# Output products of a small expert block two F tiles behind their relus, and its gathers issued from a later step

## The chip, the cores and the metric

The kernel runs on one core of a Trainium2 chip. The metric is the device time of one execution in microseconds (us). The kernel before was run three times: 393.76, 395.10 and 396.24 us, median 395.1 us. One further execution was profiled. The core has five engines, each with its own queue of instructions in program order: PE (TensorE, matrix products, its weight loads listed as PEld), DVE (VectorE), ACT (ScalarE), POOL (GpSimd) and SP (SyncE, which only issues DMAs here). They synchronise through semaphores.

## The reference

An RWKV-5 attention is followed by a mixture of experts with one expert per token.

```python
# attention: B, H, S, D = 4, 8, 768, 48; state starts at 0
for t in range(S):
    cur = einsum('bhd,bhe->bhde', u * k[t], v[t])
    y[t] = einsum('bhd,bhde->bhe', r[t], state + cur)
    state = w * state + einsum('bhd,bhe->bhde', k[t], v[t])
x = y as (B, S, H * D)                          # 3072 tokens of 384 values
# experts: E, F = 8, 1024
logits = x @ w_gate                             # (B, S, 8)
local = sigmoid(x @ w_local)
for b, s in order:
    e = argmax(logits[b, s]) if s == 0 or local[b, s] < 0.5 else previous e
    p = softmax(logits[b, s])
    out[b, s] = p[e] * (relu(x[b, s] @ w1[e]) @ w2[e])
```

Which expert a token goes to depends on the tokens before it in its batch, so the assignment is computed on the chip, and the tokens are then gathered by expert. Everything is in float32.

## The kernel before, in words

**Attention.** 16 items (4 batches by 4 pairs of heads) pass through a software pipeline (`Attention.run`), whose loop counter n goes from 0 to 16. When all heads of a batch are done, ACT issues a DMA that stores the batch's rows of x into a DRAM tile, `x_d`. Batches 0 and 1 (group 0) are complete at n = 8. In the steps that follow, the router works out the expert and the slot of each token of group 0 beside the attention of batches 2 and 3. At n = 15, `router.head` writes `gid0`, the row numbers of the first tokens of experts 0 and 1, and the callback `heads()` issues gathers for them.

**Gathers.** `Experts.gather(i)` issues one indirect DMA on POOL's queue for each 128 slots of block i: from `x_d`, by the row numbers in `gid`, into a tile `xg` (L1032). There are six `xg` tiles in turn, and a seventh gather has to wait until the tile it overwrites has been read by PE.

**Expert blocks.** `Experts.run` goes through ten blocks ("units"). Blocks 0 and 1 are small: 192 slots each for experts 0 and 1, filled from group 0 alone (`EARLY = 2`, `HEAD = 192`), so they can be computed while the router treats group 1. Blocks 2 to 9 take the eight experts by size, with 448, 424, 392, 376, 352, 336, 232 and 192 slots. Those with at least 336 slots use a scheme with fewer products (`eleven` and `seven`) and are called large here.

For a small block the loop goes over the eight F tiles m of 128 hidden features. `hidden(i, m)` computes three products into one of two PSUM buffers `h` (L1059), and ACT applies the relu into `hT` (L1062). `output(i, m)` multiplies `hT` by the second weights, three products that accumulate over m in PSUM tiles y0 to y2 (L1143). Four `hT` tiles are live at a time. `lag` says how many F tiles the output products stand behind the hidden products; it is 1 for blocks 0 and 1. Each step also runs a piece of the router for group 1 (`routing(s)`, with s = 8 i + m), and in the last steps `turn` transposes gathered tokens of the next block on PE (L1045) with a copy by DVE (L1046). The routing steps that matter here: s = 1 turns the keys of group 1 (`r.keys`), s = 8 computes row numbers of all tokens and gathers the first large block, s = 10 and s = 12 sum gates on PE (`summed`, L788), s = 14 makes one tiny product for a flag.

**Block 1** is followed by a large block (`following` is true for it alone). Its last two output products are not issued in its own loop: they are put in a list, `todo`, from which the large block takes them to fill PE. Output product 5 is issued after the loop, and output products 0 to 4 in the loop, each directly after the hidden product of the next tile. The gather of block 3 also follows the loop.

**Order.** The schedule is manual: every engine executes its instructions in the order in which the Python code emits them, and waits are derived from the tiles, buffers and DRAM regions that an instruction shares with earlier ones. Weights of block i are fetched into one of two buffers, blocks 0 and 2 onwards by SP, block 1 by ACT (`self.fetch(1, self.nc.scalar)` in block 0, step 1).

Of the kernel before, what the change touches and what calls it, by code (L numbers as in the profile page):

```python
# [26 lines left out]
DK, FK = D // P, F // P  # L27
# [9 lines left out]
EARLY = 2  # L37
# [925 lines left out]
class Experts:  # L963
# [43 lines left out]
    def bank(self, name):  # L1007
        if self.both:
            self.tp.reverse()
        return self.tp[0]  # L1010
# [291 lines left out]
    def routing(self, s):  # L1302

        r, bank = self.router, self.bank
        if s == 0:
            r.experts_of(1)
            r.shares(1)
            r.gates(0)
        if s == 1:
            r.keys(1, bank("kp1"))  # L1310
            r.runs(1)
            r.powers(1)
        if s == 2:
            r.turn_runs(1, bank("rp1"))
        if s == 3:
            r.last(1, bank("bc1"))
            r.one_hot(1)
        if s == 4:
            r.counts(1, [bank("rk1"), bank("tt1")])
            r.ranks(1)  # L1320
            r.blocks()
            r.slots(1)
            r.columns(1)
            r.numbers(1)
            r.places(1, 0)
            r.places(1, 1)
        if s == 5:
            self.fetch(EARLY, self.nc.sync)
        if s == 7:
            r.summed(1, 0)  # L1330
            r.copied(0)
        if s == 8:
            r.tokens(bank("tb1"))
            self.gather(EARLY)
            r.gates(1)
            r.weights(0)
            r.weights(1)
        if s == 10:
            r.summed(0, 1)
        if s == 12:  # L1340
            r.summed(1, 1)
            r.copied(1)
        if s == 13:
            self.flag(0)
        if s == 14:
            self.flag(1, bank("fp"))
        if s == 2 * FK:
            r.ends(bank("tb2"))

    def run(self, att, flag, ready):  # L1350
        self.flag, self.spare, self.hs = flag, att.late, None
        n = len(self.units)
        sends = []
        yb = [self.yps.tile([P, 512], F32, name=f"y{d}") for d in range(DK)]
        att.logits(B - 1, yb[0])
        for j in range(len(self.units[0]["rows"])):
            self.turn(0, j)
        att.token_logits(B - 1, yb[2])
        self.warm(2)
        self.router.powers(0)  # L1360
        later, todo, behind = [], [], None

        def fill(k=None):
            while todo and k != 0:
                todo.pop(0)()
                k = k and k - 1

        def take():
            nonlocal behind
            if behind:  # L1370
                (k, j), behind = behind, None
                todo.extend(self.seven(k, j))
                if j == FK // 2 - 1:
                    todo.append(lambda: joined(k))

        def joined(k):
            later.extend(self.join(k))
            if "yT" in self.units[k]:
                sends.extend((k, r) for r in range(2, len(self.units[k]["rows"])))
            if k + 2 < n:  # L1380
                self.fetch(k + 2, self.nc.sync)

        def drained(i):
            self.drain(i)
            sends.extend((i, j) for j in range(len(self.units[i]["rows"])))

        def then(k):
            for _ in range(min(k, len(later))):
                later.pop(0)()

        for i in range(n):
            u = self.units[i]
            after = len(self.units[i + 1]["rows"]) if i + 1 < n else 0
            following = i + 1 < n and self.units[i + 1]["seven"]
            if i == EARLY:
                self.fetch(i + 1, self.nc.sync)
                self.hs = self.spare.tile([P, 2, 3, BLOCKS[0] // 2], F32, name="hs", tag="xT")
            if u["seven"]:

                at = ["m0", "m1" if i == EARLY else "a1", "a2" if i == EARLY else "m1", "m2" if i == EARLY else "a2"][4 - after:]  # L1400

                def slot(name):
                    if (i, name) == (EARLY, "a1"):
                        self.routing(2 * FK)
                    elif name in at:
                        self.turn(i + 1, at.index(name))
                    elif sends and (i, name) > (EARLY, "b"):
                        self.send(*sends.pop(0))

                for j in range(FK // 2):  # L1410
                    if behind:
                        self.factors(*behind)
                        self.sums(*behind)
                        take()
                    then(4)
                    if j == 3 and following:
                        later.extend(self.token_sums(i + 1))
                    self.eleven(i, j, fill, lambda: slot(f"a{j}"), then)
                    behind = i, j
                    if j == 1:  # L1420
                        self.weight_sums(i, 1)
                        if i == EARLY:
                            later.extend((self.router.exceeded, lambda: self.router.halves(0), lambda: self.flag(2)))
                    if i == EARLY + 1 and j == 1:
                        later.append(lambda: self.router.halves(E - 1))
                    if j == 2 and following:
                        self.weight_sums(i + 1, 0)
                    if j == 3 and i + 2 < n:
                        self.gather(i + 2)
                    fill(max(len(todo) - 3, 0))  # L1430
                    slot(f"m{j}")
                    fill()
                continue

            lag = 3 if i and self.units[i - 1]["seven"] else 1
            for m in range(FK):
                if following and m == FK - 1:
                    self.turn(i + 1, after - 1)
                if m == 0 and behind:
                    self.factors(*behind)  # L1440
                    self.sums(*behind)
                self.hidden(i, m)
                if m == 0:
                    take()
                    fill()
                while later and m == 1:
                    later.pop(0)()
                if i == 0 and m == 0:
                    att.turn(B * HP - 1, [self.bank("tp") for _ in range(2)])
                if sends and m >= 1 and i > EARLY:  # L1450
                    self.send(*sends.pop(0))
                if m and i == n - 1:
                    self.rows(m - 1)
                elif m >= lag and not (following and m > FK - 3):
                    self.output(i, m - lag)
                if i <= EARLY:
                    self.routing(i * FK + m)
                if i == 0 and m == 1:
                    self.fetch(1, self.nc.scalar)
                if following and m == FK - 3:  # L1460
                    self.weight_sums(i + 1, 0)
                if m >= FK - after and not (following and m == FK - 1):
                    self.turn(i + 1, m - (FK - after))
            if EARLY <= i + 1 and i + 2 < n:
                self.gather(i + 2)

            if following:
                self.output(i, FK - 3)
                for step in self.token_sums(i + 1):
                    step()  # L1470
                self.both = False
                todo.extend(lambda i=i, m=m, d=d: self.output(i, m, (d,)) for m in range(FK - 2, FK) for d in range(DK))
                todo.append(lambda i=i: drained(i))
            elif i < n - 1:
                for m in range(FK - lag, FK):
                    self.output(i, m)
                drained(i)
        self.rows(FK - 1)
        self.send_rows(0)
        self.half_rows()  # L1480
        ready()
        self.send_rows(1)
# [44 lines left out]
def kernel(  # L1527
# [12 lines left out]
    nc = tc.nc  # L1540
# [28 lines left out]
    with ExitStack() as st, tc.manual_schedule():  # L1569
        ro = st.enter_context(tc.tile_pool(name="ro", bufs=1))  # L1570
        mpp = st.enter_context(tc.tile_pool(name="mpp", bufs=1, space=PSUM))
        router = Router(tc, ro, mpp, lt, mask, ident, gid, sid, gate, over[:, 0:1])
        ex = Experts(tc, st, x_d, w1, w2, out, ident, router)
        att = Attention(tc, st, rk_d, kv_d, vT_d, x_d, w_t, wp_d, kept, ident, lt, router.mp)
        att.run(router, lambda: ex.fetch(0, nc.sync), lambda: [ex.gather(i) for i in range(EARLY)])
        ex.open(st)
        router.open(1, st.enter_context(tc.tile_pool(name="ro1", bufs=1)))

# [91 lines left out]
```

## Time and profile before

| | |
|---|---|
| Median of three runs | 395.1 us (393.76 to 396.24) |
| Profiled execution | 395.21 us, of which span 393.5 us |
| Mean granted PE clock | 0.993 |
| PE busy | 375.9 us, 96% of the span |
| PEld busy | 332.1 us, 84% |
| DVE busy | 242.2 us, 62% |
| POOL busy | 143.9 us, 37% |
| ACT busy | 106.8 us, 27% |
| Hidden products of small and last blocks (L1059) | 192 records, 37.9 us |
| Output products (L1143) | 144 records, 29.2 us |
| Gathers (L1032) | 29, 30.4 us |

The span runs from the first to the last instruction of the program; the execution's own time has 1.7 us more around it. Block 0 runs from about 122 to 141 us of the span, block 1 from 141 to 161 us. A line of a timeline reads: start, duration, engine, source line, operation, output and inputs with shapes, how many were merged; in square brackets the idle time of the engine before it and what ended that. One float32 matmul of the program appears as two records, so that the three products of an F tile are six records. "Remote" as a releaser means that the profile could not tell which instruction ended the wait.

### The profile page before, as it was taken

How to read it: one execution, taken by the hardware profiler on the slowest of the kernel's cores; microseconds unless marked ns; L12 is line 12 of the kernel's file. 1: busy time of each engine (PE TensorE's matmuls, PEld its weight loads, DVE VectorE, ACT ScalarE, POOL GpSimd, SP SyncE). 2: the span in 40 equal slices, each digit the busy share in tenths (PEclk: the TensorE clock that was granted, in tenths of full speed). 3: DMA queues.
4: the chain of work that ended last, by engine and by line, in shares of the span. 5: the costliest groups of instructions: out<-in, count | busy, mean ns of one | idle time of the engine just before them, and what ended most of it. 6: DMA issues, size and time to landing. Idle time of an engine off the chain costs nothing. (4 is left out here: it accounts for less than half of the span.)

```text
span 393.5 us, 9602 instructions
## 1 busy us (share of the span) xinstructions
PE 375.9 (96%) x3856; PEld 332.1 (84%) x3856; DVE 242.2 (62%) x683; ACT 106.8 (27%) x291; POOL 143.9 (37%) x179
## 2 busy tenths in 40 slices
PE   7999999799979997999999999999999999999992
PEld 6777886686767997999999999999999999999971
DVE  7887578878834562488657647757767758440100
ACT  4132323222212111232233234224224234231110
POOL 8769999777140024310121042041242302111012
PEclk9999999999989999999999999999999999999998
DMA  7999999889122883540433064155056145173011
GB/s 255 410 411 408 410 403 322 300 285 365 47 62 93 349 327 118 215 182 3 178 96 147 22 225 182 40 217 186 22 208 226 57 162 203 41 241 133 2 35 35
DMA packets 17475, 74.98 MB, mean 191 GB/s; under 512 B 2734, under 2 KB 6591, under 8 KB 14864
## 3 DMA queue, kind: packets, MB, share of 16 engines
q1 hardware_dynamic: 10048, 56.89, 38.8%
q0 software_dynamic: 3424, 9.54, 7.1%
q10 hardware_dynamic: 3952, 7.87, 5.4%
q8 instruction: 32, 0.52, 0.5%
q14 instruction: 19, 0.16, 0.1%
HBM read 64.85 MB, written 9.54 MB: 189 GB/s over the span
## 5 line engine op out<-in xcount | busy, mean ns | idle before, releaser
L1254 POOL DMA_INDIRECT out_dram<-yo,sid x27 | 26.7, 988 | 158.8 <-ACT yo L1249 66.2
L1106 PE MATMUL h<-exT,w1t 128*128 128x224 f32 (+5 forms) x240 | 55.2, 328 | 0.0
L1032 POOL DMA_INDIRECT xg<-x_d,gid x29 | 30.4, 1048 | 63.6 <-DVE sm L870 29.0
L1110 DVE TENSOR_TENSOR hT<-h,hs 128x212 f32<-128x212 f32 (+4 forms) x60 | 21.2, 353 | 47.2 <-PE h L1106 31.3
L1106 PEld LDWEIGHTS h<-exT,w1t 128*128 128x128 f32 x240 | 41.8, 190 | 0.3 <-issue 0.3
L1059 PE MATMUL h<-exT,w1t 128*128 128x192 f32 (+1 forms) x192 | 37.9, 337 | 0.0
L288 DVE TENSOR_TENSOR am<-pair,kept 128x768 f32<-128x768 f32 x32 | 30.1, 952 | 11.8 <-PE pair L286 11.3
L1106 PE MATMUL h<-xs,ws 128*128 128x224 f32 (+5 forms) x144 | 35.4, 328 | 0.0
L1059 PEld LDWEIGHTS h<-exT,w1t 128*128 128x128 f32 x192 | 32.6, 190 | 2.2 <-issue 0.2
L220 POOL TENSOR_TENSOR pd<-rk 128x384 f32<-128x384 f32 x32 | 31.9, 1019 | 3.0 <-PE y L267 1.9
L1175 PE MATMUL y<-factors,sums 128*128 128x192 f32 x144 | 31.3, 326 | 0.0
L1143 PE MATMUL y<-hT,w2t 128*128 128x192 f32 (+1 forms) x144 | 29.2, 339 | 2.1 <-ACT hT L1062 2.1
L295 PE MATMUL y<-am,kv 128*64 128x128 f32 x384 | 28.3, 287 | 2.7 <-DVE y L271 2.6
L1046 DVE COPY exT<-tp 128x384 f32<-128x384 f32 (+7 forms) x29 | 14.1, 490 | 25.6 <-PE tp L1045 25.3
L1106 PEld LDWEIGHTS h<-xs,ws 128*128 128x128 f32 x144 | 25.5, 190 | 4.3 <-ACT hs L1113 1.2
L295 PEld LDWEIGHTS y<-am,kv 128*64 128x64 f32 x384 | 24.5, 142 | 3.5 <-DVE y L271 3.2
L1143 PEld LDWEIGHTS y<-hT,w2t 128*128 128x128 f32 x144 | 25.1, 190 | 2.8 <-ACT hT L1062 2.4
L216 POOL TENSOR_TENSOR ke<-kv,endT 128x288 f32<-128x288 f32 x32 | 24.9, 801 | 6.5 <-PE y L267 3.4
L233 POOL TENSOR_TENSOR rw<-rk,tab 128x384 f32<-128x384 f32 x26 | 23.6, 933 | 4.3 <-PE y L308 4.3
L1175 PEld LDWEIGHTS y<-factors,sums 128*128 128x128 f32 x144 | 24.7, 190 | 0.0
L286 PE MATMUL pair<-rw,kw 48*64 48x128 f32 (+1 forms) x768 | 22.6, 248 | 1.0 <-ACT end L167 0.6
L312 ACT COPY xT<-y 128x768 f32<-128x768 f32 (+1 forms) x16 | 12.5, 780 | 39.7 <-PE y L308 39.7
(276 smaller groups left out, 722.0 us busy)
## 6 DMA issues: line engine op xcount, KB each, us to landing
w1t<-in_w_dram SPq DMA_DIRECT2D x9, 1536.0 KB, 6.7
w2t<-in_w_dram SPq DMA_DIRECT2D x9, 1536.0 KB
rk<-in_rk_dram SPq DMA_DIRECT2D x15, 768.0 KB, 7.8
kv<-in_kv_dram SPq DMA_DIRECT2D x16, 584.0 KB, 8.1
vT<-in_vT_dram SPq DMA_DIRECT2D x16, 384.0 KB, 9.6
x_d<-x ACTq DMA_DIRECT2D x4, 1152.0 KB, 12.2
w1t<-in_w_dram ACTq DMA_DIRECT2D x1, 1536.0 KB
w2t<-in_w_dram ACTq DMA_DIRECT2D x1, 1536.0 KB
```

The costliest lines, as they stand in the source:

```text
L216: nc.gpsimd.tensor_mul(t["ke"][:, p::2], t["k"][:, p::2], spread(self.endT[:, p, hp], 1, C2))
L220: nc.gpsimd.tensor_mul(t["pd"][:, z], t["rT"][:, z], t["kT"][:, z])
L233: engine.tensor_mul(t["rw"][:, z], t["rT"][:, z], spread(pw, 1, z.stop - z.start))
L286: nc.tensor.matmul(sc[f * DP:(f + 1) * DP, h, i, x:], lhsT=t["kw"][q, c, o * DP:(o + 1) * DP], rhs=t["rw"][q, c, x:], start=True, stop=True)
L288: return lambda: nc.vector.tensor_mul(t["am"][:, g], sc, spread(self.kept[:, g:g + 3], 1, 2))
L295: nc.tensor.matmul(t["y"][p * DP:(p + 1) * DP, h, c2 * P:(c2 + 1) * P], lhsT=t["v"][:, (2 * c + h) * DH:(2 * c + h) * DH + DP], rhs=t["am" ...
L1032: self.nc.gpsimd.indirect_dma_start(out=xg[:n], out_offset=None, in_=self.x_d[:rows], in_offset=bass.IndirectOffsetOnAxis(ap=u["gid"][:n, ...
L1059: nc.tensor.matmul(h[:, :n], lhsT=u["w1"][:, m, kk, :], rhs=u["xT"][:, kk, :], start=(kk == 0), stop=(kk == DK - 1))
L1106: nc.tensor.matmul(out, lhsT=a, rhs=b, start=start and k == 0, stop=stop and k == len(terms) - 1, skip_group_check=True)
L1143: nc.tensor.matmul(u["y"][d][:, :n], lhsT=u["w2"][:, m, d * P:(d + 1) * P], rhs=u[m], start=(m == 0), stop=(m == FK - 1))
L1175: return lambda: nc.tensor.matmul(bank[:, x * half:(x + 1) * half], lhsT=a, rhs=b, start=(j == 0 and x == 0), stop=(j == FK // 2 - 1), ski ...
L1254: self.nc.gpsimd.indirect_dma_start(out=out.rearrange("n (h d) -> (n h) d", h=2) if half else out, out_offset=bass.IndirectOffsetOnAxis(ap ...
```

## The change

Two edits. First, `heads()` at n = 15 gathers block 0 alone, and block 1's gather is called from `routing(1)`, in the second step of block 0. Second, in block 1 no output product is issued in step 3; from step 4 the output products stand two F tiles behind, so that steps 4, 5 and 6 issue output products 2, 3 and 4. Output product 5 remains behind the loop, and 6 and 7 remain in `todo`.

```diff
@@ routing(s)
         if s == 1:
+            self.gather(1)
             r.keys(1, bank("kp1"))
             r.runs(1)
             r.powers(1)
@@ run, loop over m of a small block
                 if m and i == n - 1:
                     self.rows(m - 1)
-                elif m >= lag and not (following and m > FK - 3):
-                    self.output(i, m - lag)
+                elif m >= lag and not (following and m in (3, FK - 1)):
+                    self.output(i, m - lag - (following and m > 3))
@@ the kernel's body
-        att.run(router, lambda: ex.fetch(0, nc.sync), lambda: [ex.gather(i) for i in range(EARLY)])
+        att.run(router, lambda: ex.fetch(0, nc.sync), lambda: ex.gather(0))
```

## Prediction

> **What bounds the kernel now.** I read the page first, then the table of waits, then the timeline around the two places that the diff touches, then the same stretches cut into windows.
>
> From the page of the kernel before:
>
> ```profile
> span 393.5 us, 9602 instructions
> PE 375.9 (96%) x3856; PEld 332.1 (84%) x3856; DVE 242.2 (62%) x683; ACT 106.8 (27%) x291; POOL 143.9 (37%) x179
> L1032 POOL DMA_INDIRECT xg<-x_d,gid x29 | 30.4, 1048 | 63.6 <-DVE sm L870 29.0
> ```
>
> TensorE (PE) has work for 96% of the span, so only what fills or opens a hole in PE moves the end. The chain that ended last names only the final scatter and says nothing about the middle. Weights come 1,536 KB at a time and land 6.7 us after their issue (the page's median), while a large block takes some 25 us, so no transfer bounds that stage.
>
> From the table of waits (us in total, times, longest):
>
> ```profile
> ACT hT L1062 <- remote: 7.3, 2, 6.1
> PEld y L1143 <- ACT hT L1062: 2.4, 1, 2.4
> PE y L1143 <- ACT hT L1062: 2.1, 1, 2.1
> ```
>
> Output products (L1143) wait for a relu (L1062) exactly once in the whole kernel, for 2.1 us, and that relu itself waited for something that the profile cannot name. The timeline shows where: in the second small block.
>
> ```profile
> 147.15 1.24 PE L1059 MATMUL h<-exT,w1t 128*128 128x192 f32 x6
> 148.22 1.14 PE L1143 MATMUL y<-hT,w2t 128*128 128x192 f32 x6
> 149.20 1.14 PE L1059 MATMUL h<-exT,w1t 128*128 128x192 f32 x6
> 149.93 1.00 POOL L1032 DMA_INDIRECT xg<-x_d,gid  x1 [0.31 <-issue]
> 151.23 1.00 POOL L1032 DMA_INDIRECT xg<-x_d,gid  x1 [0.30 <-issue]
> 152.02 0.33 ACT L1062 ACTIVATE hT<-h 128x192 f32<-128x192 f32 x1 [6.14 <-remote]
> 152.40 1.24 PE L1143 MATMUL y<-hT,w2t 128*128 128x192 f32 x6 [2.07 <-ACT hT L1062]
> 153.50 0.33 ACT L1062 ACTIVATE hT<-h 128x192 f32<-128x192 f32 x1 [1.15 <-remote]
> ...
> 154.37 0.55 PE L1045 MATMUL tp<-ident,xg 128*128 128x128 f32 x3
> ```
>
> Hidden product 3 ended at 148.39, yet its relu began at 152.02: 3.6 us late, on an idle ScalarE. Number 4 ended at 150.34 and its relu began at 153.50, 3.2 us late. In quiet stretches a relu follows its product by 0.1 us (product 2: end 145.45, relu 145.54). The late stretch falls inside a run of six gathers on GpSimd (144.70 to 152.23). PE, which had run out of permitted work at 150.34, stood until 152.40.
>
> The first four gathers show the same thing. In the windows, cut at 112, 113, 114, 115, 116, PE did nothing from 112.42 to 114.58, and then worked at half clock:
>
> ```profile
> 112.50:113.00 0.50, 0.00 (x0) 0.00 (x0) 0.00 (x0) 0.00 (x0) 0.50 (x1) 1.00 0.97 203
> 115.00:116.00 1.00, 1.00 (x14) 1.00 (x12) 0.55 (x2) 0.00 (x0) 0.71 (x1) 0.50 0.65 187
> ```
>
> (After the stretch: its length, busy us of PE, PEld, DVE, ACT and POOL, granted PE clock, DMA share, GB/s.) There `y<-y,vT` (L271) began at 113.56 though its matmuls (L267) had ended at 111.49.
>
> **What the Trainium skill says.** "TensorE: Matmul & The Clock Gate", Part 1: PE's clock is halved after a mostly idle window of about 3.4 us. The trace agrees: 0.50 granted from 114.62 to 118.03, 3.41 us, after 2.15 us of idleness; the 2.06 us at 150.34 did not trip it. The same page, "Architectural detail", on queue depths: GpSimd executes its queue strictly first in, first out. The trace fits: 29 gathers start in program order. "Perfetto Trace Analysis", "Per-instruction lifecycle": a matmul's recorded end is estimated, and the semaphore update after it is outside the record. So a late relu can mean a late signal; the trace agrees that such a gap exists, 3.6 us here, but no page explains it. "DMA: Bandwidth & Descriptors", "SWDGE vs HWDGE vs iDMA": a GpSimd DMA's descriptors are computed by its own cores; the trace has 1.05 us for one gather.
>
> **Part 1, the gathers of the second small block.** In the source, two of four gathers move from the attention's last step but one to the first block's second step. But an instruction moves in time only if its place among its own engine's instructions moves, or if it acquires a wait. In the order of the two built programs, GpSimd's queue is the same row for row: four gathers follow `pd`, the first waits for DVE's `gid` and one DMA, the others wait for nothing, and the next row is the large block's gather. Between the old place and the new one GpSimd is given no other instruction. The rows they read (batches 0 and 1) are not those that the last `x_d` store writes, so no wait appears. SP's queue is also identical. Hence these two gathers still run at 113.46 and 114.77: two instructions times 1.0 us moved by 0. Their DMAs stay too, and are not pushed into the 3 MB weight fetch that ScalarE issues at 125.25. Cost and gain 0. Were they to move after all: at most the first stall's 2.15 us and half of 3.41 us, 3.9 us, saved; at worst another such stall, 3.9 us, paid.
>
> **Part 2, the output products.** Nothing is added or removed; PE gets the same matmuls in another order. Writing h, o for hidden and output products of an F tile, r for the routing sums, t for turning a gathered tile:
> before: h3 o2 h4 o3 r t0 h5 o4 t1 h6 t2 t3 h7 o5
> after: h3 h4 o2 r t0 h5 o3 t1 h6 o4 t2 t3 h7 o5
>
> Durations, start to start: six records of h or o 0.98 us (148.22 to 149.20), r 0.79 (153.58 to 154.37), t0 0.38 (154.37 to 154.75), plus 0.09 of change-over before r. In both programs the first instruction that needs relu 3 is stuck until 152.40: before it is o3, after it is h5, whose PSUM buffer is the one h3 used (there are two).
>
> - Before, PE's permitted work ran out (next possible start) at 150.17. Lost: 152.40 - 150.17 = 2.23 us.
> - After: h3 at 147.15 as now, h4 148.22, o2 149.20, r 150.26, t0 151.06, out of work at 151.44. Lost: 152.40 - 151.44 = 0.96 us.
> - Gain: 2.23 - 0.96 = 1.27 us, which is r and t0 with their change-over brought under the wait.
>
> Is what comes early ready? o2 needs relu 2, done at 145.87. r needs `val`, done on DVE at 146.66. t0 needs the large block's first gather: GpSimd's own wait on that landing passed at 150.62, 0.44 us ahead of t0. If it were later, t0 would only use up idle time up to 0.96 us.
>
> New waits: h4, h5 and h6 now each wait directly for the relu two tiles before. Behind them on PE stand all later products. h4 waits for relu 2 (long done). h6 would start near 154.8 and needs relu 4, done at 153.83: 0.9 us of margin. h7 needs relu 5, which even 3.6 us late (153.4 + 3.6 + 0.3 = 157.3) meets h7 at about 157.4. The four live `hT` buffers suffice: relu 6 overwrites tile 2, whose product is done at m = 4. Elsewhere a 0.98 us product covers a relu of 0.33 us plus 0.1, so two tiles of lag gain nothing where signals are prompt.
>
> Does the gain reach the end? PE has no hole over 0.15 us from 152.40 to the end, so the large blocks begin 1.27 us earlier. Their weights are not late: the third fetch waits for h7 itself and shifts along, with 6.7 us to landing against a block of 25. What is late next is nothing until the final scatters.
>
> **Sum.** The profiled execution took 395.2 us (span 393.5 and 1.7 around it), the median of the three runs is 395.1, so I subtract from either: 395.2 - 1.27 = 393.9. The runs scatter from 393.8 to 396.2, as much as the gain.
>
> **Rivals.**
> 1. Likeliest, as worked: the signal is late until a given time, set by GpSimd's run of gathers. For it: the second late update (relu 4) came at 153.4, while PE was busy, so PE need not be idle to be heard. 393.9. Chance 0.50.
> 2. The late signal follows PE's idleness: it came 1.1 and 1.6 us after PE had stopped (112.42, 150.34). Then filling PE to 151.44 pushes relu 3 to about 153.3, and the same 2.2 us are lost. Gain 0, 395.1. Also the outcome if other executions hardly have the stall. Chance 0.23.
> 3. The wait is shorter in most executions than in the profiled one (relu 3 before 151.4), so the new order hides all: 395.2 - 2.2 = 393.0. Chance 0.10.
> 4. Slower: t0 done early frees its buffer 3 us sooner, so a seventh gather joins the run at 152.5 instead of 155.19. If that prolongs the silence, PE idles from 151.44 until relu 3 comes. From relu 3 at about 153.9 on (an idle stretch like the 2.15 us of 112.42) the clock halves for 3.41 us. Price with relu 3 at 154.0: idle 154.4 - 151.4 = 3.0, minus the 2.2 of now, plus 1.7: 2.5 us, 397.7. Against it: relu 3's signal arrived at 151.9, before that gather. Chance 0.12.
> 5. The gathers move after all (4 us either way), or something unseen. Chance 0.05.
>
> **Range and chances.** From rival 3 with half a microsecond of run scatter, 392.5, to no gain at the slow end of the runs shown, 396.3; the slower rival and half of the rest stay outside, 0.15. About 1%, 4 us, is what a measurement of this kernel can tell from no change. No case above but the fifth reaches it by itself: faster 0.03, same 0.92, slower 0.05, the slow side for the halved clock coming on top of a bad draw.
>
> **What will show it.** Right: gathers near 110.6, 112.2, 113.5 and 114.8 as before, PE idle again at 112.4; h4 directly after h3; PE's hole in the second block about 1 us, ended by relu 3 and in front of an h (L1059) rather than an o (L1143). Wrong: the hole still 2 us (rival 2), a half-clock window near 152 (rival 4), or gathers of the second block after 120 us (part 1).

## The result, and the profile after

| | before | after |
|---|---|---|
| Median | 394.32 us (14 runs, 391.38 to 396.24) | 394.62 us (14 runs, 391.38 to 396.33) |
| Ratio | 1 | 1.0006, 95% interval 0.9984 to 1.0028 |
| Profiled execution | 395.21 us, span 393.5 | 393.52 us, span 391.8 |

The change makes no difference that can be measured. The forecast of 393.9 us lies 0.2% below the measured median and the range of 392.5 to 396.3 holds it, but the gain of 1.27 us behind the forecast isn't there. That the time fits is no proof of the reasoning: the gain is smaller than the scatter of the runs, the range takes in no gain at all, and with 14 runs the kernel before itself stands 0.8 us below its first three. Ratios are formed over all runs counted and can differ a little from the quotient of the medians.

Two lines of the page of the changed kernel; the prediction shows the same two of before:

```profile
PE 376.8 (96%) x3856; PEld 331.9 (85%) x3856; DVE 238.2 (61%) x683; ACT 106.9 (27%) x291; POOL 144.2 (37%) x179
L1032 POOL DMA_INDIRECT xg<-x_d,gid x29 | 30.5, 1051 | 62.1 <-DVE sm L870 27.1
```

From its table of waits (us in total, times, longest):

```profile
ACT hT L1062 <- remote: 7.2, 2, 6.1
...
PEld mp L788 <- issue: 3.0, 4, 1.3
```

Two relus still wait for a releaser without a name, for as long as before (7.3 us then). The rows in which output products (L1143) waited for a relu are gone. In their place the routing sums (L788) wait for "issue", which means nothing that the profile shows. The timeline of the second small block:

```profile
145.14 2.22 PE L1059 MATMUL h<-exT,w1t 128*128 128x192 f32 x12
...
147.19 1.14 PE L1143 MATMUL y<-hT,w2t 128*128 128x192 f32 x6
...
148.26 0.64 PE L788 MATMUL mp<-ohq,val 128*32 128x128 f32 x15
149.18 0.27 PE L788 MATMUL mp<-ohq,val 128*32 128x128 f32 x1 [0.28 <-issue]
...
149.90 0.39 PE L788 MATMUL mp<-ohq,val 128*32 128x128 f32 x3 [0.45 <-issue]
150.00 0.33 ACT L1062 ACTIVATE hT<-h 128x192 f32<-128x192 f32 x1 [6.13 <-remote]
150.61 0.27 PE L788 MATMUL mp<-ohq,val 128*32 128x128 f32 x1 [0.32 <-issue]
...
151.33 0.42 PE L788 MATMUL mp<-ohq,val 128*32 128x128 f32 x4 [0.45 <-issue]
151.45 0.33 ACT L1062 ACTIVATE hT<-h 128x192 f32<-128x192 f32 x1 [1.12 <-remote]
...
151.69 0.55 PE L1045 MATMUL tp<-ident,xg 128*128 128x128 f32 x3
```

The new order is there: both hidden products (12 records from 145.14), then o2, then the routing sums r. But r, which needs no relu and took 0.79 us before, takes from 148.26 to 151.69, 3.43 us. From 149 us on PE gets its instructions out in dribbles about 0.72 us apart (149.18, 149.90, 150.61, 151.33), though the profile shows nothing that they wait for; `val` and `ohq`, which r reads, are written before 145 us. The relus are set free in the same stretch. So PE isn't idle for want of permitted work: it is held itself.

Where the time went can be measured without holes, from the starts of the relus (L1062) in the ACT records and the first gather of all: one stretch from the first gather to relu 0 of block 0, one through block 0, and one from relu 0 to relu 7 of block 1, the block whose order changed.

| us | first gather to relu 0 | block 0 | block 1, relu 0 to 7 | span |
|---|---|---|---|---|
| before | 12.80 | 19.11 | 17.86 | 393.5 |
| after | 10.98 | 19.10 | 18.16 | 391.8 |

Block 1 is 0.30 us longer after the change, in one profiled execution of each kernel. That this profiled execution is nevertheless 1.7 us shorter comes from the stretch ahead of block 0 (1.82 us), which the change left as it was: its hole was 1.41 us instead of 2.15 (112.24 to 113.66), and PE's clock stayed whole behind it. A window of the changed kernel, with the columns explained in the prediction:

```profile
114.00:118.00 4.00, 4.00 (x57) 2.66 (x54) 1.18 (x3) 0.52 (x2) 1.25 (x2) 1.00 0.29 78
```

The granted clock is 1.00 where it was 0.50 before. Executions differ in this, as the experiments below show.

### The profile page after: what moved, and what is told of

It is laid out like the page before. It is cut to its first block, busy times and chain, and to the rows that moved or that the text cites. A ratio compares the mean times of both kernels' runs of the same rounds, so it can differ in the third digit from the quotient of the medians.

```text
span 391.8 us, 9602 instructions
## 1 busy us (share of the span) xinstructions
PE 376.8 (96%) x3856; PEld 331.9 (85%) x3856; DVE 238.2 (61%) x683; ACT 106.9 (27%) x291; POOL 144.2 (37%) x179
## 5 line engine op out<-in xcount | busy, mean ns | idle before, releaser
L1143 PE MATMUL y<-hT,w2t 128*128 128x192 f32 (+1 forms) x144 | 29.1, 338 | 0.0
L1143 PEld LDWEIGHTS y<-hT,w2t 128*128 128x128 f32 x144 | 25.1, 190 | 0.4
```

The costliest lines, as they stand in the source:

```text
L1143: nc.tensor.matmul(u["y"][d][:, :n], lhsT=u["w2"][:, m, d * P:(d + 1) * P], rhs=u[m], start=(m == 0), stop=(m == FK - 1))
```

## The experiments

The runs were made in four sets, each on another chip, with the kernel before beside it. Line numbers in the variants are shifted by up to eight. The sets differ, and this became the first finding:

| set | kernel before, median | first gather to relu 0 | block 1, relu 0 to 7 |
|---|---|---|---|
| the result above | 394.32 us | 12.80, 10.98 | 17.86, 18.16 |
| first set | 389.14 us (23 runs) | 9.67 to 9.68 (four kernels) | 15.52 to 15.53 |
| second set | 388.89 us (26 runs) | 9.67 to 9.68 (four kernels) | before 15.52, after 15.53 |
| third set | 392.56 us (39 runs) | 10.14, 10.84 | see below |
| fourth set | 391.98 us (25 runs) | 10.15, 10.91 | see below |

One theory and two rivals at the start. G: GpSimd's run of gathers holds back PE's messages (the semaphore updates that tell other engines that a product is done) and then PE itself; this is called the silence of PE below. The rivals: D, the gathered bytes on their way beside the weights do it; I, PE's own order or its instruction fetches do.

**First set: take the gathers away, on another queue, shorten the run, space it.** In the first two, the gathers of blocks 2 and 3 become plain DMAs of fixed rows (their values, and so the output, change), on SP or on GpSimd:

```diff
             xg = self.gp.tile([P, D], F32, name="xg")
+            if EARLY <= i <= EARLY + 1:
+                t = (i - EARLY) * 512 + (c - u["cols"][0]) * P
+                self.nc.sync.dma_start(out=xg[:n], in_=self.x_d[t:t + n])   # or gpsimd
+                u["xg"].append(xg)
+                continue
```

> The changed kernel, with the token gathers of the third and fourth blocks (those that GpSimd issues one behind the other while the second small block's products run) replaced by plain DMAs of fixed rows of x on SP's queue: the same bytes and the same tiles, other tokens, so the output is not the reference's. The gathers of the first two blocks stay on GpSimd. Theory G (GpSimd's run of gathers holds back PE's messages and then PE itself): the routing sums of the second block take 0.8 us instead of 3.4, the relus of hidden products 3 and 4 start within 0.3 us of the products' end instead of 3.6 us late, and from the start of hidden product 3 to the start of output product 5 it takes 10.6 us instead of 13.3; the first block's stall near 112 us stays (1.4 to 2.2 us). Rival D (the gathered bytes' way through the DMA engines beside the 3 MB of weights): the bytes are the same, so the stall stays at 2 us or more. Rival I (PE's own order or its fetches of instructions): the stall stays at 2 to 2.6 us.

> As the run before it, but the plain DMAs of fixed rows are issued on GpSimd's queue, behind a copy of one column that waits for the token numbers as the gathers did; the output is not the reference's. Theory G in its narrow form (only the indirect gathers, about 1.05 us of GpSimd's work each, do it): no stall, 10.6 us from hidden product 3 to output product 5. Theory G in its wide form (any DMA whose descriptors GpSimd writes does it): PE's messages are late again, by as much of 2.6 us as GpSimd's issues are long beside a gather's 1.3 us pace. Rivals D and I: the stall stays at 2 to 2.6 us.

The third has `bufs=4` instead of 6 in the pool of gathered tokens; the fourth has a `gpsimd.memset` behind each of block 2's gathers.

> The changed kernel with four buffers for gathered tokens instead of six: in the second small block GpSimd then issues four gathers in a row and has to wait for a turn before the fifth. Theory G: the silence ends with the run, some 2.6 us earlier: PE loses at most 1.2 us instead of 2.6 there, so the kernel is 1 to 2.5 us shorter than the changed one, if the fourth block's late gathers delay nothing (they are turned some 10 us later at the earliest). Rivals D and I: the loss stays at 2 to 2.6 us; the time is that of the kernel before, 394.3, or later by what the late gathers cost.

> The changed kernel with a fill of 128x960 on GpSimd behind each of the third block's four gathers, so that the gathers stand about 2 us apart instead of 1.3. Theory G, if it takes gathers back to back: messages get out in the pauses, no relu is over 1 us late, PE loses under 1 us. Theory G, if it takes any gather: the same loss per gather, 2 us or more, spread over the longer run. Rival I: 2 to 2.6 us lost at the same instructions as before.

Measured: 388.04 and 388.34 us with plain DMAs, 389.51 us with the fills (one run each), against 389.14 before. Four buffers: 388.95 us, ratio 0.9999 (0.9983 to 1.0016). In none of the four is a relu late or r stretched, and block 1 takes 15.52 or 15.53 us in all. But the first stall, which none of them touched, is absent too: a hole of 0.22 us near 111 us. Nothing was silenced in this set, so it tells none of the theories apart. All four expectations took the stall for a property of the kernel. What follows is only that four buffers cost nothing where there is no stall.

**Second set: both kernels again, and a relu that is truly late.** The kernels as they are, to see whether the stall belongs to them:

> The kernel before, unchanged, looked at again, because the four runs ahead of this show no stall in either small block, not even the first block's, which none of them touched, and the kernel before took 389.1 us beside them instead of 394.3. Theory C (the silence of PE comes and goes with the chip or the execution and isn't made by the kernel's order): where it is absent, this has no hole of PE over 0.4 us near 112 and 145 us, and its span is near 387 us. Rival V (the four variants had no stall because of what they changed): PE has a hole of about 2 us in the second small block and one near 112 us again.

> The changed kernel, unchanged. Theory C: where there is no stall, nothing is there to be hidden; the second small block's PE work is the same, so the ratio to the kernel before is 1.000, within 0.2%, and its profile has no hole in the routing sums. The prediction's view (the relus are late and the new order hides 1.27 us of it) : 1.27 us faster, ratio 0.9967, and before it a hole in the kernel before.

Measured: before 388.68 us in its run; after 389.43 us, ratio 1.0008 (0.9983 to 1.0032). No relu is late in either. The changed kernel's timeline in this set:

```profile
143.91 2.22 PE L1059 MATMUL h<-exT,w1t 128*128 128x192 f32 x12
...
145.25 0.33 ACT L1062 ACTIVATE hT<-h 128x192 f32<-128x192 f32 x1 [2.61 <-PE h L1059]
145.97 1.14 PE L1143 MATMUL y<-hT,w2t 128*128 128x192 f32 x6
146.22 0.33 ACT L1062 ACTIVATE hT<-h 128x192 f32<-128x192 f32 x1 [0.64 <-PE h L1059]
...
147.03 0.86 PE L788 MATMUL mp<-ohq,val 128*32 128x128 f32 x24
147.83 0.55 PE L1045 MATMUL tp<-ident,xg 128*128 128x128 f32 x3
```

Each relu names its product as releaser, and r takes 0.80 us. Block 1 takes 15.52 us before and 15.53 after. Where signals are prompt, the order of the output products is worth nothing, as the prediction said of other places. The stall accounts for most of what the sets differ by: taking what the profiled execution of before lost in its two stretches (12.80 - 9.68 = 3.12 and 17.86 - 15.52 = 2.34) from its span of 393.5 leaves 388.0, against 387.0 for the same kernel here.

Since the late signal had gone, I made the relu late by other means: ACT gets eight copies ahead of relu 3 of block 1, in the old order and in the new. PE's program isn't touched; GpSimd fills the copied tile once, at the start of the kernel.

```diff
+        if (i, m) == (1, 3):
+            for _ in range(8):
+                nc.scalar.copy(self.router.pad, self.router.pad)      # 128x768, float32
         nc.scalar.activation(self.kept(i, m), h[:, :n], Act.Relu)
```

> The kernel before, with eight copies of 128x768 (0.80 us each) on ACT ahead of relu 3 of the second small block, so that this relu is truly late, by some 3.9 us, while PE is left alone. The prediction's step (PE sits still until relu 3): PE's hole ahead of output product 3 is 2.2 to 2.8 us, and the kernel is that much longer than the kernel before. Rival: some of it is hidden and the hole is under 1 us.

> The changed kernel with the same eight copies ahead of relu 3. The prediction's step (the routing sums and the first turn run under the wait, then hidden product 5 waits for product 3's PSUM buffer): a hole of 1.0 to 1.5 us ahead of hidden product 5, and 1.27 us (1.1 to 1.4) less than the run before it. Rival S (PE can't run on past the waiting product, whatever is late): PE stops inside the routing sums, and the two late kernels are equal within 0.4 us.

Timeline of the old order with the late relu, and windows of the same kernel behind the hole:

```profile
143.14 6.86 ACT L1066 COPY pad<-pad 128x768 f32<-128x768 f32 x8
...
149.91 0.55 ACT L1067 ACTIVATE hT<-h 128x192 f32<-128x192 f32 x2
...
150.29 1.71 PE L1148 MATMUL y<-hT,w2t 128*128 128x192 f32 x6 [2.58 <-ACT hT L1067]
```

```profile
151.00:152.00 1.00, 1.00 (x8) 0.56 (x10) 0.00 (x0) 0.00 (x0) 0.00 (x0) 0.50 0.05 18
152.00:153.00 1.00, 1.00 (x21) 0.92 (x24) 0.00 (x0) 0.00 (x0) 0.00 (x0) 0.50 0.00 0
153.00:154.00 1.00, 1.00 (x13) 0.64 (x4) 0.00 (x0) 0.27 (x1) 0.00 (x0) 0.50 0.00 0
```

Timeline of the new order with the late relu:

```profile
147.93 0.86 PE L790 MATMUL mp<-ohq,val 128*32 128x128 f32 x24
148.73 0.55 PE L1047 MATMUL tp<-ident,xg 128*128 128x128 f32 x3
150.21 0.54 ACT L1067 ACTIVATE hT<-h 128x192 f32<-128x192 f32 x2
...
150.59 1.24 PE L1061 MATMUL h<-exT,w1t 128*128 128x192 f32 x6 [1.31 <-ACT hT L1067]
```

Here PE does run r and the first turn under the wait, and then stands ahead of hidden product 5 until relu 3 is done, as the prediction had it. The hole shrinks from 2.58 us to 1.31: by 1.27 us, the forecast's own term to the hundredth. Rival S, that PE can't run past the wait, is out for a wait of this kind. The times are 394.21 us (ratio 1.0131, 1.0102 to 1.0159; 4 runs) and 391.71 us (1.0068, 1.0043 to 1.0093; 11 runs). In time both expectations missed. The old order is 5.3 us above the kernel before and not 2.2 to 2.8, and the medians differ by 2.5 us and not by 1.27. The longer hole goes with a halved clock of PE (0.50 in the windows above, 1.00 throughout in the new order). Block 1 takes 19.94 us in the old order, 4.42 above the undisturbed 15.52: 2.58 for the hole, and 1.84 beyond it, of which half speed over some 3.4 us makes about 1.7 (an estimate from the windows). In the new order it takes 17.11 us, 1.58 above the undisturbed 15.53: 1.31 for the hole, and only 0.27 beyond it.

**Third set: part 1 as it was meant, and a shorter delay.** A copy on GpSimd that reads block 0's relu 0 makes block 1's two gathers really wait:

```diff
         if s == 1:
+            self.nc.gpsimd.tensor_copy(r.pad, self.units[0][0][:, :1])
             self.gather(1)
```

> The changed kernel, with a copy of one column of the first block's relu 0 on GpSimd ahead of the second block's two gathers, so that these really are issued in the first block's second step, which the change alone did not bring about. The prediction's part 1: in the changed kernel they ran at their old place, near 114 us; here they run near 120 and 121.5 us. Where PE is not silenced near 112 us there is nothing to be saved: the ratio to the kernel before is 1.000 within 0.3%. Where it is silenced, two gathers instead of four stand there and the first block's stall shrinks by up to 2 us, 3.9 with the halved clock. Rival: their landing beside the 3 MB weight fetch of 125 us makes the second block's first turn late, and the kernel is over 1 us longer.

The other is the kernel before with `range(6)` in place of `range(8)`.

> The kernel before with six copies on ACT ahead of relu 3 instead of eight, 1.72 us less delay by the copies' measured 0.86 us each. With eight, PE's hole was 2.58 us and its clock was halved behind it, and the stretch from relu 0 to relu 7 of the second block took 4.4 us more than undisturbed. Theory H (the halved clock is what the hole costs beyond its own length): a hole of 0.8 to 0.9 us, no halved clock, and the stretch takes 0.8 to 1.1 us more than the undisturbed 15.5. Rival: the stretch takes 1.6 us or more above it, because something else than the clock was lost behind the hole.

In this set PE is silenced again. Timeline of the moved gathers:

```profile
109.64 1.27 POOL L1033 DMA_INDIRECT xg<-x_d,gid  x1 [10.28 <-DVE gid L820]
111.21 0.99 POOL L1033 DMA_INDIRECT xg<-x_d,gid  x1 [0.31 <-issue]
...
112.15 1.09 PE L295 MATMUL y<-am,kv 128*64 128x128 f32 x12 [0.69 <-DVE y L271]
...
120.92 1.03 POOL L1033 DMA_INDIRECT xg<-x_d,gid  x1 [0.55 <-issue]
122.26 0.96 POOL L1033 DMA_INDIRECT xg<-x_d,gid  x1 [0.30 <-issue]
...
148.15 0.38 PE L789 MATMUL mp<-ohq,val 128*32 128x128 f32 x2 [0.65 <-issue]
```

With two gathers in the run instead of four, the first stall costs 0.46 us (10.14 against the undisturbed 9.68); with four it cost 1.16 (10.84) in the other kernel of this set. The two gathers near 121 us cost nothing: block 0 takes 19.11 us as everywhere. Block 1, whose run of six is as in the changed kernel, takes 17.39 us, 1.9 too much, with r interrupted again (last line), this time after 22 of its 24 matmuls and not after 15. PE's program is the same in both, so the stop has no fixed place in it. The time is 391.57 us, ratio 0.9983 (0.9965 to 1.0000): 0.7 us less than before, with an interval from nothing to 1.4. The rival, a late first turn in block 1, isn't seen.

The shorter delay came out mixed. Its timeline:

```profile
150.35 0.33 ACT L1067 ACTIVATE hT<-h 128x192 f32<-128x192 f32 x1
...
150.72 1.24 PE L1148 MATMUL y<-hT,w2t 128*128 128x192 f32 x6 [0.86 <-issue]
...
151.90 1.31 PE L790 MATMUL mp<-ohq,val 128*32 128x128 f32 x24
152.84 0.33 ACT L1067 ACTIVATE hT<-h 128x192 f32<-128x192 f32 x1 [2.17 <-remote]
```

The hole is 0.86 us and the clock stays at 1.00, as theory H had it. But block 1 takes 17.10 us, 1.58 above 15.52 and not 0.8 to 1.1: relu 4 is late for a "remote" reason and r takes 1.24 us to the next instruction instead of 0.79. This set has the silence, so the test of H is spoilt; that the halved clock is most of the excess in the second set rests on that set alone, on its windows and on the 1.84 us against 0.27. The time says something else: 392.40 us, ratio 1.0000 (0.9980 to 1.0019). Six copies of 0.86 us ahead of a relu cost nothing that can be measured here. That this relu would have been held up anyway is the likely reason; no profile of the kernel before was taken in this set.

**Fourth set: both cures together, and plain DMAs with a control.** The first kernel has the moved gathers and four buffers. The second is the one of the first set, measured again in the hope of a set with the silence.

> Both cures together: the second block's two gathers really moved to the first block's second step (as in the run that took 0.9983 of the time before), and four buffers for gathered tokens instead of six, so that no run of GpSimd's gathers is longer than two near 110 us and four near 141 us. Theory G (it is the run of gathers that silences PE): relu 0 to relu 7 of the second block takes 15.5 to 16.3 us even where the kernel before loses 1.5 to 2.6 us there, and the first stall loses at most 0.5 us; the ratio to the kernel before is 0.993 to 0.997 where PE is silenced, 1.000 where it is not. Rival W (the silence doesn't follow the length of the run): the stretch takes 17 us or more as with six buffers, ratio 0.998.

> The changed kernel with the third and fourth blocks' token gathers replaced by plain DMAs of fixed rows on SP's queue, once more; the output is not the reference's. Theory G: where PE is silenced near 112 us (the four gathers there are untouched and serve as the control), it is not in the second block: relu 0 to relu 7 takes 15.5 us. Rival D (the bytes and their way beside the weights): 17 us or more, with late relus. If the first stall is absent too, the run says nothing on this.

Timeline of the kernel with plain DMAs:

```profile
116.49 1.73 PE L295 MATMUL y<-am,kv 128*64 128x128 f32 x22 [1.42 <-issue]
...
149.23 0.33 ACT L1067 ACTIVATE hT<-h 128x192 f32<-128x192 f32 x1 [2.61 <-PE h L1064]
149.94 1.14 PE L1148 MATMUL y<-hT,w2t 128*128 128x192 f32 x6
150.21 0.33 ACT L1067 ACTIVATE hT<-h 128x192 f32<-128x192 f32 x1 [0.65 <-PE h L1064]
151.01 0.86 PE L788 MATMUL mp<-ohq,val 128*32 128x128 f32 x24
```

The control works: the four untouched gathers near 113 us go with a hole of 1.42 us (first line; first gather to relu 0 takes 10.91 us). In the same execution the second block, with the same PE order and the same bytes but no gathers on GpSimd, takes 15.53 us, and every relu is prompt. Rivals D and I would have it at 17 us or more. The bytes don't come at exactly the same moments: the first plain DMA is issued at 142.59 us, 0.7 us ahead of relu 0, where the first gather of the changed kernel came 2.2 us behind it. But they are under way beside the weights: the DMA engines' busy share is 0.91 to 1.10 in each microsecond from 146 to 151. The time is 389.84 us, ratio 0.9940 (0.9915 to 0.9964). The profiled execution is the slowest of its 16 (392.69 us): near 71 us, far from any gather, PE waits 2.28 us for DVE and then runs at a clock of 0.50, so the length of the block is read from this profile and the time from the median. Two things stay open. One is whether it is GpSimd's work on a gather or the form of its transfers (one row of a token after another instead of a block of rows): the variant with plain DMAs on GpSimd would have told, but ran only in the first set. The other is the path by which PE is reached; that gathers delay PE's fetches of instructions, for one, was not tested.

Both cures together: 389.75 us, ratio 0.9932 (0.9908 to 0.9955). By the ratio this is 2.7 us (1.8 to 3.6) less than the kernel before, by the medians 2.2, and so less than the changed one too, which is equal to it within about 0.3% in both sets that timed it. Which of the two cures gives how much wasn't measured in one set. From its timeline:

```profile
147.91 1.08 PE L789 MATMUL mp<-ohq,val 128*32 128x128 f32 x24
148.60 0.55 ACT L1063 ACTIVATE hT<-h 128x192 f32<-128x192 f32 x2 [5.08 <-remote]
148.91 0.55 PE L1046 MATMUL tp<-ident,xg 128*128 128x128 f32 x3
```

Two relus are still late together. Relu 3 comes 5.77 us after the first gather of the run (142.83), no earlier than in the third set's kernel with a run of six, where it was 5.75 (146.82 - 141.07). What the shorter run spares is what followed there: relu 4 came 1.4 us behind relu 3, and PE stood for 0.65 and 0.43 us. Here the run ends at 147.72, both relus come 0.9 us later, in time for hidden product 5, and r takes 1.00 us up to the first turn. Block 1 takes 15.73 us, 0.2 above the undisturbed value, and the first stall costs 0.47. Rival W (17 us or more) is out.

## Why the prediction was right in time and wrong in its reason

- **Bound, and where the holes are.** Right for the profiled execution. What it couldn't see from one profile is that they come and go: four variants of the changed kernel in the first set and both kernels in the second show none.
- **Part 1 moves nothing.** Right. The gathers start at 110.42, 112.00, 113.29 and 114.60 us, as before, and PE stands again at 112.24. Made to move, they take 0.7 us off the first stall (10.84 to 10.14 in the third set), not 3.9; the bound was for an execution with the clock halved.
- **When relu 3 comes.** Right. It came 7.32 us after the first gather of the run before (152.02 - 144.70) and 7.31 after (150.00 - 142.69), relu 4 8.80 and 8.76 after. These two alone can't tell gathers from place in the program, since the run starts 2.19 us after relu 0 in both. The pair of the third and fourth sets can: 5.75 and 5.77 us after the first gather, but 7.93 and 8.45 after relu 0. In the first of the two it came at 146.82 while PE had not stood still yet (its first hole opens after 147.5). So relu 3 follows the gathers and not PE's idleness; rival 2's mechanism is wrong though its outcome, no gain, is what happened. How long after the first gather it comes differs between sets.
- **The step that failed: "r and t0 with their change-over brought under the wait".** It took for granted that PE, while its signals are late, still works through whatever the program permits. The lost time was forecast to fall from 2.23 to 0.96 us; it went from 2.34 to 2.63 in block 1. The hole of about 1 us in front of a hidden product, named beforehand as the sign of being right, isn't there. PE stopped inside r, 6.2 us after the first gather of the run (148.90 - 142.69), where in the old order it had run out of work at 5.6 (150.34 - 144.70). The late-relu pair shows that the working itself, order, durations and PSUM buffer, was exact: 1.27 us, if the relu is late and PE is free. The prediction had read the silence as a late message from PE, when it held PE as well. Whether the products of the late relus were only reported late or really ended late, the trace can't say, since the ends of matmuls are estimated in it, as the prediction notes. The first stall gave no hint of this. There PE waits for a result of DVE (L271), which the profile before names as what ended the hole; L271 itself starts late, and PE goes on 0.05 us after its end, before the change (114.53 to 114.58) and after it:

```profile
112.64 0.97 DVE L271 TENSOR_TENSOR y<-y,vT 128x768 f32<-128x768 f32 x1 [1.32 <-PE pair L321]
113.66 1.95 PE L295 MATMUL y<-am,kv 128*64 128x128 f32 x24 [1.41 <-issue]
```

- **Rival 3** (all hidden) and **rival 4** (a longer silence and half the clock) didn't occur in the changed kernel; no clock below 1.00 follows block 1's stall. The price of rival 4's clock is borne out by the second set, where half the clock for some 3.4 us followed a hole of 2.58 us and not one of 1.31. The Trainium skill, "TensorE: Matmul & The Clock Gate", Part 1, has the clock halved after an idle window of about 3.4 us; "mostly idle" is the prediction's own wording. Here shorter holes were enough, and their length alone doesn't decide: 2.15 us near 112 us in the profile before, and 2.28 us near 71 us in that of the fourth set's plain DMAs, were followed by a clock of 0.50; one of 2.22 us near 71 us in the profile before was not (1.00 behind it).
- **No effect at the end of the span** beyond the block itself: from relu 7 to the end both kernels take 233.1 to 233.2 us.

## What to carry to other kernels

A wait without a named releaser, on an engine whose input is finished by the profile, says that a message was late or that the input was; before work is moved under it, look whether the sender itself runs on in that stretch, and whether the stall is there in a second execution. The gain of a reordering is worth testing by making the awaited step late on purpose: here that returned the forecast difference of the two holes to 0.01 us and so put the fault elsewhere. And remove the cause rather than cover it: fewer gathers in a row on GpSimd gave about 2.7 us where moving matmuls gave nothing.

## What the runs showed of the hardware that was not expected

- During a run of indirect gathers on GpSimd, 1.3 us apart, the relus that wait for PE's products can come 3.2 to 3.6 us late and PE itself issues only in dribbles every 0.72 us, though it waits for nothing in the program. Ahead of block 0, two gathers in a row cost 0.46 to 0.47 us and four 1.16 to 1.30 (3.1 with the clock halved); in block 1, four cost 0.2 and six 1.9 to 2.6.
- The same program shows it in some sets of runs and not in others: the median of the kernel before was 394.3, 392.6 and 392.0 us in sets where a profile showed it, 389.1 and 388.9 where none did. GpSimd's gathers look the same in both (1.00 us each, 1.3 apart). Why is open; each set ran on one chip, and nothing tried here separates the chip from other circumstances of a set.
